# A fused DFT and two-layer MLP on one core: four float32 second stages for eight, two jobs moved to GpSimd, and the second transform one step sooner

## The chip, the core and the metric

The kernel runs on one core of a Trainium2 chip. The metric is the device time of one execution in microseconds (us). Before the change it is 877.92 us, the median of three runs between 877.84 and 877.99.

TensorE (PE in the profile; its weight loads are PEld) multiplies, VectorE (DVE) and ScalarE (ACT) do the elementwise work, GpSimd (POOL) does some more of it and issues a few DMAs, and SyncE (SP) issues the other DMAs. Each engine works through its own instructions in the order in which the program issued them; semaphores tie them together.

## The reference

```python
x: (4, 3008, 256) float32;  w_in: (256, 2048);  w_out: (2048, 256)
X = np.fft.fft(x, axis=1); X = np.fft.fft(X, axis=2)
t = X.real.reshape(12032, 256)
h = t @ w_in
g = h * (1.0 / (1.0 + np.exp(-h)))
return g @ w_out
```

## The kernel before, in words

The transform along the 256 features is folded into w_in at the start (lines 517 to 547), so that x has only to be transformed along the sequence. Symmetries of the real transform reduce that to `operand` (lines 251 to 326), which adds and subtracts folded rows of x, and `transform` (lines 328 to 358), one set of matrix products with cosine and sine tables (tiles te, to, t2). There are 16 such transforms, four for each of the four batches. `spread` (lines 368 to 388) takes the result of one out of PSUM into the tiles uvh and uvl, and copies one row of it over all 128 partitions with a DMA into the tile ub.

The MLP then runs over 13 chunks of columns: four of 376 or 378 columns and nine of 502. A chunk has 16 groups f of 128 hidden features. The main loop (lines 732 to 778) has one step n for each chunk and group; chunk 0 is steps 0 to 15, chunk 1 begins at step 16. A step issues, in this order:

- `first` (lines 404 to 412): six products into a PSUM tile pq, of which there are two;
- `second` of the group three steps back (LAG is 3): into four PSUM tiles acc;
- in some steps a transform (a "turn"), which takes a pq tile of its own;
- `act` (lines 417 to 436): three VectorE instructions (L421, L422, L423) from pq to the tile h, then the step's list `fills`, then Silu and a copy to gh on ScalarE;
- the step's list `after`, `rest` of the group before (L447 on VectorE, gl = h - gh), `spread` after a turn, the step's `plan`, and pieces of two work queues: `queue` (operands and `split_wo`) and `pool_queue` (`fold_sums`, `fold_diffs`, and the low part xl of an operand, L323).

The float32 numbers are multiplied as a high and a low part: three products for one (gh by woh, gh by wol, gl by woh; L464, L465, L471). In the first FULL = 8 groups of chunk 0 the second stage is made in plain float32 instead, as one product that the hardware runs in two passes (L462), without gh, gl and L447. The weights w_out for it are the four tiles `wo_f32`, which `split_wo` splits into high and low parts later (L123 on ScalarE, L125 on VectorE).

w_out comes as eight blocks q of 16-bit halves. `load_wo` fetches a block, `upper_wo` (ScalarE, L78) and `lower_wo` (VectorE, L82) put the halves together, and for the blocks that aren't needed in float32 `high_wo` (ScalarE, L115) and `low_wo` (VectorE, L118) split them. Block q is needed by the second stages of groups 2q and 2q+1. The lists `after` and `fills` (lines 722 to 730) say in which step each of these is issued.

The rows of x of the first batch are kept raw until `first_x1` (lines 195 to 211) adds their mirrored rows, the tiles minus; its last three additions (L210) run on VectorE in steps 2 and 3. `fold_diffs` (lines 213 to 247, GpSimd and ScalarE) uses the sums.

The order of work is written out by hand: `begins` gives the step in which the work on an operand begins, `turns` the step of its transform.

Of the kernel before, what the change touches and what calls it, by code (L numbers as in the profile page):

```python
# [24 lines left out]
F32 = mybir.dt.float32  # L25
# [7 lines left out]
ALU = mybir.AluOpType  # L33
PSUM = bass.MemoryType.PSUM

B, S, D, DFF = 4, 3008, 256, 2048
# [6 lines left out]
STARTS = [sum(CHUNKS[:j]) for j in range(len(CHUNKS))]  # L43
LAST = len(CHUNKS) - 1
LAG = 3
FULL = 8
NF = DFF // 128


# [1 line left out]
def fft_mlp(ctx, tc, x1, x2, x2_first, w_in, w_out, te, to, t2, t2f, rot1, rot2, dft, out):  # L51
    nc = tc.nc
    ctx.enter_context(tc.manual_schedule())
    tt = nc.vector.tensor_tensor
# [3 lines left out]
    fold_p = ctx.enter_context(tc.tile_pool(name="fold", bufs=1))  # L58
# [14 lines left out]
    def load_raw(t, block):  # L73
        nc.sync.dma_start(out=t[:, 1:1 + 8 * D].rearrange("p (c n) -> p c n", c=2), in_=block)

    def upper(dst, raw):
        flat = dst.rearrange("p c n -> p (c n)")
        nc.scalar.activation(flat.bitcast(F16)[:, 1::2], raw.bitcast(BF16)[:, 4:4 + 8 * D:4], AF.Copy)  # L78

    def lower(dst, raw):  # L80
        t = dst.rearrange("p c n -> p (c n)").bitcast(U32)
        stt(t, raw.bitcast(U32)[:, 1:1 + 4 * D:2], 13, t, op0=ALU.logical_shift_right, op1=ALU.bitwise_or)  # L82

    wo = [[wts.tile([128, 2, D], F32R, name=f"woh{f}") for f in range(NF // 2)], {}]
    wo_f32 = [wts.tile([128, 2, D], F32, tag="wof", name="wof", bufs=FULL // 2 + 1) for _ in range(FULL // 2)]
    for q in range(FULL // 2, NF // 2):
        wo[1][q] = wts.tile([128, 2, D], F32R, name=f"wol{q}")
# [4 lines left out]
    wo_raw, wo_wide = {}, {}  # L92

    def load_wo(q):
        if 3 <= q < 7:
            t = wr.tile([128, RAW], U16, tag="win", name="wo", bufs=4)
        else:
            tag = ("ri0", "xh", "xl")[q] if q < 3 else "ri1"
            t = (xs if tag[0] == "x" else fold_p).tile([128, RAW], U16, tag=tag, name="wo")
        wo_raw[q] = t  # L100
        load_raw(t, w_out[q * 256:(q + 1) * 256, :].bitcast(U16).rearrange("(f p) d -> p f d", p=128))

    def upper_wo(q):
        if q < FULL // 2:
            wo_wide[q] = wo_f32[q]
        else:
            wo_wide[q] = fold_p.tile([128, 2, D], F32, tag="half", name="wf", bufs=3)
            nc.gpsimd.memset(wo_wide[q], 0.0)
        upper(wo_wide[q], wo_raw[q])

    def lower_wo(q):
# [3 lines left out]
        nc.scalar.activation(wo[0][q], wo_wide[q], AF.Copy)  # L115

    def low_wo(q):
        tt(wo[1][q], wo_wide.pop(q), wo[0][q].bitcast(F32), op=ALU.subtract)  # L118

    def split_wo(q):  # L120
        wf, wh = wo_f32[q], wo[0][q]
        wl = wo[1][q] = wts.tile([128, 2, D], F32R, tag="wof", name="wol", bufs=FULL // 2 + 1)
        nc.scalar.activation(wh, wf, AF.Copy)  # L123
# [21 lines left out]
    def fold_tile(name, k, i):  # L145
        if (name, k, i) not in folded:
            folded[name, k, i] = fold_p.tile([128, 2, 2, D], F32, tag=f"{name}{k}", name=name)
        return folded[name, k, i]
# [22 lines left out]
    minus = {}  # L171
# [23 lines left out]
    def first_x1(h, x3, dd):  # L195
        g, sm = raw_x[0, 0, h], fold_tile("sm", 0, 0)[:, h]
        if h == 0:
            tt(g[:, 0:2], g[:, 0:2], minus[h, 0], op=ALU.add)
        tt(sm, g[:, 0:2], g[:, 2:4], op=ALU.add)
        if h:  # L200
            tt(sm, sm, minus[h, 0], op=ALU.add)
        yield
        tt(sm, sm, minus[h, 1], op=ALU.add)
        tt(dd, sm[:, 0], sm[:, 1], op=ALU.subtract)
        nc.scalar.activation(x3[:, h, ends], dd[:, ends], AF.Copy)
        tt(x3[:, h, 1:128], dd[:, 1:128], dd[:, 129:], op=ALU.add)
        tt(x3[:, 1 - h, 129:], dd[:, 1:128], dd[:, 129:], op=ALU.subtract)
        yield
        for j in range(1 - h, 2):
            tt(g[:, 2 * j:2 * j + 2], g[:, 2 * j:2 * j + 2], minus[h, j], op=ALU.add)  # L210
            yield

    def fold_diffs(k, i):
        tt = nc.gpsimd.tensor_tensor
        rot = rot_sb[k]
        gs = [raw_x.pop((k, i, h)) for h in range(2)]

        def differences(g):
            tt(g[:, 0:2], g[:, 0:2], g[:, 2:4], op=ALU.subtract)
            even, odd = g[:, 0:2, 1:128], g[:, 0:2, 129:]  # L220
            tt(g[:, 2:4, 1:128], even, odd, op=ALU.add)
            tt(g[:, 2, 129:], even[:, 1], odd[:, 1], op=ALU.subtract)
            tt(g[:, 3, 129:], odd[:, 0], even[:, 0], op=ALU.subtract)

        def turned(h, g):
            ri = fold_tile("ri", k, i)
            nc.scalar.activation(g[:, 2:4, ends], g[:, 0:2, ends], AF.Copy)
            for j in range(2):
                nc.scalar.activation(g[:, j], g[:, 3], AF.Copy, scale=rot[:, h, 1 - j:2 - j])
                nc.scalar.activation(ri[:, h, j], g[:, 2], AF.Copy, scale=rot[:, h, j:j + 1])  # L230

        def sums(h, g):
            ri = fold_tile("ri", k, i)
            for j, op in ((0, ALU.subtract), (1, ALU.add)):
                tt(ri[:, h, j], ri[:, h, j], g[:, j], op=op)  # L235

        differences(gs[0])
        yield 9
        differences(gs[1])
        yield 9  # L240
        turned(0, gs[0])
        yield 9
        sums(0, gs[0])
        turned(1, gs[1])
        yield 9
        sums(1, gs[1])
        ready.add(("ri", k, i, 128))
# [169 lines left out]
    def act(c, f, fill=()):  # L417
# [6 lines left out]
        for fn, q in fill:  # L424
            fn(q)
        if c == 0 and f < FULL:
            g = gp.tile([128, 2, CH], F32, tag=("gh", "gl")[f % 2], name="g")
# [12 lines left out]
    def rest(c, f):  # L440
        if c == 0 and f < FULL or (c, f) in rested:
            return
        rested.add((c, f))
        gh, gl, g = gs[c, f]
        n = chunks[c][3]
        for sg in signs(c, f):
            tt(gl[:, sg, :n], g[:, sg, :n], gh[:, sg, :n].bitcast(F32), op=ALU.subtract)  # L447
# [41 lines left out]
    queue, pool_queue = [], []  # L489
# [103 lines left out]
    x3 = xf[:, :768].rearrange("p (a d) -> p a d", a=3)  # L593
    x2_work = first_x2(x3)
    x1_work = [first_x1(h, x3, xf[:, 768 + 256 * h:1024 + 256 * h]) for h in range(2)]

    def product(a, i):
# [19 lines left out]
    for q in range(3):  # L617
        load_wo(q)
# [16 lines left out]
    product(0, 0)  # L635
    lower(wf32[4], win.pop(4))
    load_wo(3)
    project(4)
    next(x1_work[1])
# [7 lines left out]
    small(1)  # L647
    lower(wf32[5], win.pop(5))
    load_wo(4)
    project(5)  # L650
    first_spread = spread_first(po)
# [11 lines left out]
    upper(wf32[7], win[7])  # L663
    small(4)
    lower(wf32[7], win.pop(7))
    load_wo(6)


    def first_row():
# [8 lines left out]
    def at(j, f, fn, *a):  # L678
        j, f = j + f // NF, f % NF
        plan.setdefault((j, f), []).append((fn, a))  # L680
# [1 line left out]
    def add(q, name, work):  # L682
        q.append((name, work))

    turns, begins = {}, {1: (0, 4), 2: (1, 7), 3: (2, 0), 4: (2, 14), 5: (3, 3), 6: (3, 15)}
    for c in range(1, 4):
        turns[c - 1, 12] = c
    for b in range(1, B):
        j, c = 3 * b + 1, 4 * b
        for k, when in enumerate(((j - 1, 0 if b > 1 else 3), (j - 1, 12 if b > 1 else 11), (j, 8), (j + 1, 4))):  # L690
# [11 lines left out]
        at(j, f + 5 - (j < 3), add_x, k, i, *ps)  # L702
        at(j, f + 8 - (j < 3), add, pool_queue, (name, k, i), {"sm": fold_sums, "ri": fold_diffs}[name](k, i, *ps))

    at(0, 8, add, pool_queue, ("ri", 0, 0), fold_diffs(0, 0))
    for h in range(2):
        at(0, 11 + 2 * h, load_x, 1, 0, every, (h,))
        at(0, 15 + 2 * h, add_x, 1, 0, every, (h,))
# [4 lines left out]
    for b in range(1, B - 1):  # L713
        j = 3 * b + 1
# [5 lines left out]


    after, fills = {}, {}
    for q, n in enumerate((0, 1, 2, 3, 4, 5, 5, 7)):
        after.setdefault(n, []).append((upper_wo, q))
        fills.setdefault(n + 1, []).append((lower_wo, q))
        if q == 6:
            fills[n + 1].append((load_tables, q))
        if q >= FULL // 2:
            after.setdefault(n + 1, []).append((high_wo, q))
            fills.setdefault(n + 2, []).append((low_wo, q))  # L730

    for n in range(len(steps) + LAG):
        c, f = steps[min(n, len(steps) - 1)]
# [151 lines left out]
```

## Time and profile before

| | |
|---|---|
| median of three runs | 877.92 us |
| the profiled execution | 878.42 us |
| its span, first to last instruction | 876.7 us |
| mean granted TensorE clock | 1.000 of full speed |
| PE busy | 867.5 us (99%) |
| VectorE busy | 708.1 us (81%) |
| ScalarE busy | 507.0 us (58%) |
| GpSimd busy | 188.5 us (21%) |
| chain that ended last, by engine | PE 88%, DMA 4%, DVE 4%, ACT 2%, POOL 1% |

The shares are means over the whole span. Starts of matmuls are measured and their ends are modelled, so steps of TensorE are best read from start to start. A chain's share tells which engine each moment waited for; a wait that the profile shows in brackets behind an instruction is the idle time of its engine just before it, and who ended it.

### The profile page before, as it was taken

Reading aid. Unit: us, or ns where it says so; the run is one execution under the profiler, and the core shown is the slowest. Engines: PE = TensorE matmul, PEld = TensorE weight load, DVE = VectorE, ACT = ScalarE, POOL = GpSimd, SP = SyncE. Lnnn points to the kernel's source line nnn. Section 1 sums busy time; section 2 is a strip of 40 time slices with the busy share of each in tenths; the row PEclk is TensorE's granted clock in tenths of the full one; section 3 lists DMA queues with packets and bytes.
Section 4 is the critical chain, followed back from the end, with each engine's and each line's share of the span. In section 5 each row is a group of like instructions: output and inputs, shape, how many; then the busy total and the mean of one; then the engine's idle time right before and its main releaser. Section 6 shows DMA issues by size and latency. Waiting matters only on the chain.

```text
span 876.7 us, 11030 instructions
## 1 busy us (share of the span) xinstructions
PE 867.5 (99%) x4130; PEld 749.6 (86%) x4130; DVE 708.1 (81%) x1000; ACT 507.0 (58%) x644; POOL 188.5 (21%) x236
## 2 busy tenths in 40 slices
PE   8999999999999999999999999999999999999998
PEld 6779999999998888888888888888888888888886
DVE  5998988888897887889778777888877887777774
ACT  4676757555765565557566555557546556455544
POOL 3335531303522120243312310050200110000000
PEclk9999999999999999999999999999999999999999
DMA  9644343236131433224225201323011021200101
GB/s 337 229 160 73 97 71 54 37 58 93 8 97 37 68 85 58 37 17 106 41 19 135 9 1 49 56 48 57 1 7 50 0 10 48 10 0 4 44 1 47
DMA packets 22838, 51.71 MB, mean 59 GB/s; under 512 B 3585, under 2 KB 12161, under 8 KB 22401
## 3 DMA queue, kind: packets, MB, share of 16 engines
q1 hardware_dynamic: 19344, 37.58, 19.9%
q0 software_dynamic: 3440, 13.44, 7.7%
q8 instruction: 32, 0.52, 0.2%
q14 instruction: 22, 0.17, 0.1%
HBM read 35.77 MB, written 12.34 MB: 55 GB/s over the span
## 4 chain that ended last, share of the span: by engine, by line
PE 88%; DMA 4%; DVE 4%; ACT 2%; POOL 1%; issue 1%; SPq 0%; ACTq 0%; DVEq 0%
PE acc L471 19%; PE acc L465 19%; PE acc L464 19%; PE pq L410 9%; PE pq L412 9%; PE pq L411 9%; PE pq L341 5%; DMA ub<-row 1%; DMA x_t<-in_x_first_dram 1%; DMA win<-in_w_in_dram 1%; DMA wo<-in_w_out_dram 1%; POOL xl L323 1%; DVE h L421 1%; DVE h L422 1%; DVE wf L82 0%
## 5 line engine op out<-in xcount | busy, mean ns | idle before, releaser
L434 ACT ACTIVATE h<-h 128x1004 f32<-128x1004 f32 (+3 forms) x202 | 197.6, 978 | 304.3 <-DVE h L423 301.2
L464 PE MATMUL acc<-gh,woh 128*128 128x502 f32 (+2 forms) x800 | 299.4, 374 | 0.6 <-ACT o L479 0.6
L465 PE MATMUL acc<-gh,wol 128*128 128x502 f32 (+2 forms) x800 | 299.5, 374 | 0.0
L447 DVE TENSOR_TENSOR gl<-h,gh 128x1004 fp32r<-128x1004 f32 (+3 forms) x202 | 236.2, 1170 | 16.0 <-ACT gh L435 15.9
L421 DVE SCALAR_TENSOR_TENSOR h<-ub,a,pq 128x502 f32<-128x502 f32 (+2 forms) x208 | 144.8, 696 | 95.9 <-PE pq L412 89.4
L471 PE MATMUL acc<-gl,woh 128*128 128x502 f32 (+2 forms) x800 | 208.8, 375 | 0.0
L435 ACT ACTIVATE gh<-h 128x1004 fp32r<-128x1004 f32 (+3 forms) x202 | 197.6, 978 | 6.4
L465 PEld LDWEIGHTS acc<-gh,wol 128*128 128x128 f32 x800 | 151.1, 189 | 22.6
L464 PEld LDWEIGHTS acc<-gh,woh 128*128 128x128 f32 x800 | 150.4, 188 | 23.3 <-ACT o L479 0.9
L471 PEld LDWEIGHTS acc<-gl,woh 128*128 128x128 f32 x800 | 148.2, 188 | 22.9
L410 PE MATMUL pq<-uv,abh 128*128 128x502 f32 (+2 forms) x416 | 158.1, 380 | 0.1
L411 PE MATMUL pq<-uv,abh 128*128 128x502 f32 (+2 forms) x416 | 154.8, 372 | 0.0
L412 PE MATMUL pq<-uv,abl 128*128 128x502 f32 (+2 forms) x416 | 154.7, 372 | 0.0
L422 DVE TENSOR_TENSOR h<-h,pq 128x502 f32<-128x502 f32 (+2 forms) x208 | 132.7, 638 | 7.2
L423 DVE TENSOR_TENSOR h<-h,pq 128x502 f32<-128x502 f32 (+2 forms) x208 | 132.6, 637 | 7.2
L323 POOL TENSOR_TENSOR xl<-xf,xh 128x256 fp32r<-128x256 f32 x53 | 53.5, 1039 | 370.9 <-ACT xh L316 327.4
L410 PEld LDWEIGHTS pq<-uv,abh 128*128 128x128 f32 x416 | 78.2, 188 | 12.6 <-DVE h L423 0.7
L411 PEld LDWEIGHTS pq<-uv,abh 128*128 128x128 f32 x416 | 78.3, 188 | 11.9
L412 PEld LDWEIGHTS pq<-uv,abl 128*128 128x128 f32 x416 | 78.2, 188 | 11.2
L235 POOL TENSOR_TENSOR ri<-ri,raw 128x256 f32<-128x256 f32 x24 | 22.9, 971 | 55.3 <-ACT ri L230 55.1
L479 ACT ACTIVATE o<-acc 128x502 f32<-128x502 f32 (+2 forms) x52 | 27.6, 558 | 9.7 <-PE acc L471 7.6
L388 DVE TENSOR_TENSOR uv<-pq,uv 128x752 fp32r<-128x752 f32 (+4 forms) x21 | 14.5, 716 | 20.5 <-ACT row L384 20.4
(114 smaller groups left out, 476.7 us busy)
## 6 DMA issues: line engine op xcount, KB each, us to landing
raw<-in_x_dram SPq DMA_DIRECT2D x20, 512.0 KB, 5.5
raw<-in_x_dram POOLq DMA_DIRECT2D x18, 512.0 KB, 7.3
out_dram<-o SPq DMA_DIRECT2D x36, 251.0 KB, 2.1
win<-in_w_in_dram SPq DMA_DIRECT2D x8, 512.0 KB, 7.9
wo<-in_w_out_dram SPq DMA_DIRECT2D x8, 512.0 KB, 8.0
out_dram<-o SPq DMA_DIRECT2D x12, 188.0 KB, 2.4
ub<-row SPq DMA_DIRECT2D x8, 188.0 KB, 8.6
te<-in_te_dram POOLq DMA_DIRECT2D x1, 1128.0 KB, 5.9
```

Source lines behind the costliest of these rows:

```text
L410: nc.tensor.matmul(po, abh[:, i, fs], uvh[:, i, :n], start=True, stop=False)
L411: nc.tensor.matmul(po, abh[:, i, fs], uvl[:, i, :n], start=False, stop=False)
L412: nc.tensor.matmul(po, abl[:, i, fs], uvh[:, i, :n], start=False, stop=True)
L421: stt(p[:, :n], ub[:, :n], a128[f // 2][:, f % 2:f % 2 + 1], pq[:, 0, :n], op0=ALU.mult, op1=ALU.add)
L422: tt(h[:, 0, :n], p[:, :n], pq[:, 1, :n], op=ALU.add)
L423: tt(h[:, 1, :n], p[:, :n], pq[:, 1, :n], op=ALU.subtract)
L434: nc.scalar.activation(h[:, sg, :n], h[:, sg, :n], AF.Silu)
L435: nc.scalar.activation(gh[:, sg, :n], h[:, sg, :n], AF.Copy)
L447: tt(gl[:, sg, :n], g[:, sg, :n], gh[:, sg, :n].bitcast(F32), op=ALU.subtract)
L464: nc.tensor.matmul(po, wo[0][f // 2][:, f % 2, es], gh[:, sg, :n], start=f == 0, stop=False)
L465: nc.tensor.matmul(po, wo[1][f // 2][:, f % 2, es], gh[:, sg, :n], start=False, stop=False)
L471: nc.tensor.matmul(accs[c][i][:, :n], wo[0][f // 2][:, f % 2, es], gl[:, sg, :n], start=False, stop=f == NF - 1)
```

## The change

- FULL is 4: the second stages of groups 4 to 7 of chunk 0 are made of three products, with gh, gl and L447. Two blocks of w_out are kept in float32 and split later in place of four; six are split at once in place of four.
- `low_wo` (the subtraction L118) and the last three additions of `first_x1` (L210) run on GpSimd in place of VectorE. The clearing of the tiles for w_out's blocks, on GpSimd before and after, gets a place of its own, one step ahead of `upper_wo`.
- The blocks 6 and 7 of w_out are put together at steps 7 and 9 and the steps after them (before: 5 and 7). Block 6 is loaded in step 1, into another buffer, and no longer in the prologue.
- The work on operand 1 begins in step 2 (before: 4), and its transform is issued in step 11 (before: 12). The first `fold_diffs` is queued in step 9 (before: 8).

```diff
-FULL = 8
+FULL = 4
 def load_wo(q):
-    if 3 <= q < 7:
+    if 3 <= q < 6:
         t = wr.tile([128, RAW], U16, tag="win", name="wo", bufs=4)
     else:
-        tag = ("ri0", "xh", "xl")[q] if q < 3 else "ri1"
+        tag = {0: "ri0", 1: "xh", 2: "xl", 6: "ri0", 7: "ri1"}[q]
...
+def clear_wo(q):
+    wo_wide[q] = fold_p.tile([128, 2, D], F32, tag="half", name="wf", bufs=3)
+    nc.gpsimd.memset(wo_wide[q], 0.0)
+
 def upper_wo(q):
     if q < FULL // 2:
         wo_wide[q] = wo_f32[q]
-    else:
-        wo_wide[q] = fold_p.tile([128, 2, D], F32, tag="half", name="wf", bufs=3)
-        nc.gpsimd.memset(wo_wide[q], 0.0)
     upper(wo_wide[q], wo_raw[q])
...
 def low_wo(q):
-    tt(wo[1][q], wo_wide.pop(q), wo[0][q].bitcast(F32), op=ALU.subtract)
+    nc.gpsimd.tensor_tensor(wo[1][q], wo_wide.pop(q), wo[0][q].bitcast(F32), op=ALU.subtract)
...
     for j in range(1 - h, 2):
-        tt(g[:, 2 * j:2 * j + 2], g[:, 2 * j:2 * j + 2], minus[h, j], op=ALU.add)
+        p = g[:, 2 * j:2 * j + 2]
+        nc.gpsimd.tensor_tensor(p, p, minus[h, j], op=ALU.add)
         yield
...
     lower(wf32[7], win.pop(7))
-    load_wo(6)
...
-turns, begins = {}, {1: (0, 4), 2: (1, 7), ...}
+turns, begins = {}, {1: (0, 2), 2: (1, 7), ...}
 for c in range(1, 4):
-    turns[c - 1, 12] = c
+    turns[c - 1, 12 if c > 1 else 11] = c
...
-at(0, 8, add, pool_queue, ("ri", 0, 0), fold_diffs(0, 0))
+at(0, 9, add, pool_queue, ("ri", 0, 0), fold_diffs(0, 0))
...
-for q, n in enumerate((0, 1, 2, 3, 4, 5, 5, 7)):
+for q, n in enumerate((0, 1, 2, 3, 4, 5, 7, 9)):
     after.setdefault(n, []).append((upper_wo, q))
     fills.setdefault(n + 1, []).append((lower_wo, q))
-    if q == 6:
+    if q == 0:
+        fills[n + 1].append((load_wo, 6))
+    if q == 5:
         fills[n + 1].append((load_tables, q))
     if q >= FULL // 2:
+        fills.setdefault(n - 1, []).append((clear_wo, q))
         after.setdefault(n + 1, []).append((high_wo, q))
         fills.setdefault(n + 2, []).append((low_wo, q))
```

## Rows read from the trace of the kernel before

**Rows 1.** Stretches: us; busy PE, PEld, DVE, ACT, POOL; clock; DMA share, GB/s.
```profile
40.00:60.00 20.00, 20.00 (x80) 14.18 (x79) 19.51 (x43) 12.13 (x20) 3.01 (x7) 1.00 0.33 123
...
400.00:600.00 200.00, 200.00 (x910) 167.82 (x909) 160.09 (x207) 115.97 (x139) 48.23 (x52) 1.00 0.25 46
```
**Rows 2.** Timeline, weight loads that open steps: start us, duration us, instruction.
```profile
45.06 0.19 PEld L410 LDWEIGHTS pq<-uv,abh 128*128 128x128 f32 x1
...
48.60 0.19 PEld L410 LDWEIGHTS pq<-uv,abh 128*128 128x128 f32 x1
...
62.80 0.19 PEld L410 LDWEIGHTS pq<-uv,abh 128*128 128x128 f32 x1
...
66.04 0.19 PEld L410 LDWEIGHTS pq<-uv,abh 128*128 128x128 f32 x1
...
69.15 0.58 PEld L341 LDWEIGHTS pq<-te,xh 128*128 128x128 f32 x4
...
72.55 0.19 PEld L410 LDWEIGHTS pq<-uv,abh 128*128 128x128 f32 x1
```
**Rows 3.** Timeline of VectorE, steps 2 to 11.
```profile
37.16 0.68 DVE L82 SCALAR_TENSOR_TENSOR wof<-wo,wof 128x512 uint32<-128x512 uint32 x1
...
37.76 1.29 DVE L210 TENSOR_TENSOR raw<-raw,minus 128x512 f32<-128x512 f32 x2
...
41.85 0.61 DVE L421 SCALAR_TENSOR_TENSOR h<-ub,a,pq 128x376 f32<-128x376 f32 x1
...
43.54 0.70 DVE L82 SCALAR_TENSOR_TENSOR wof<-wo,wof 128x512 uint32<-128x512 uint32 x1
...
44.14 0.70 DVE L275 TENSOR_TENSOR sm<-sm 128x512 f32<-128x512 f32 x1
...
61.38 0.94 DVE L447 TENSOR_TENSOR gl<-h,gh 128x752 fp32r<-128x752 f32 x1
...
66.17 0.59 DVE L421 SCALAR_TENSOR_TENSOR h<-ub,a,pq 128x376 f32<-128x376 f32 x1
```
**Rows 4.** Timeline around the row's DMA and the start of chunk 1.
```profile
75.99 0.34 SPq L138 DMA_DIRECT2D raw<-in_x_dram  x1
...
76.42 0.55 SPq L385 DMA_DIRECT2D ub<-row  x1
...
86.13 0.61 DVE L421 SCALAR_TENSOR_TENSOR h<-ub,a,pq 128x378 f32<-128x378 f32 x1 [2.10 <-DMA ub<-row]
...
93.21 0.44 PE L464 MATMUL acc<-gh,woh 128*128 128x378 f32 x1 [0.59 <-ACT o L479]
```
**Rows 5.** Timeline of VectorE and GpSimd, three places where both work.
```profile
65.02 1.22 DVE L125 TENSOR_TENSOR wol<-wof,woh 128x512 fp32r<-128x512 f32 x1
...
70.31 1.28 POOL L219 TENSOR_TENSOR raw<-raw 128x512 f32<-128x512 f32 x1
...
70.68 1.71 DVE L447 TENSOR_TENSOR gl<-h,gh 128x752 fp32r<-128x752 f32 x1
...
71.67 1.31 POOL L221 TENSOR_TENSOR raw<-raw 128x254 f32<-128x254 f32 x1
...
206.01 1.29 POOL L219 TENSOR_TENSOR raw<-raw 128x512 f32<-128x512 f32 x1 [5.32 <-DMA raw<-in_x_dram]
207.38 1.06 POOL L221 TENSOR_TENSOR raw<-raw 128x254 f32<-128x254 f32 x1
...
206.66 1.19 DVE L275 TENSOR_TENSOR sm<-sm 128x512 f32<-128x512 f32 x1
207.87 1.13 DVE L278 TENSOR_TENSOR sm<-sm 64x512 f32<-64x512 f32 x1
```
**Rows 6.** Timeline of GpSimd: the clearing of w_out's tiles, and xl.
```profile
36.14 1.45 POOL L108 MEMSET wf<- 128x512 f32 x3
...
61.52 5.32 POOL L323 TENSOR_TENSOR xl<-xf,xh 128x256 fp32r<-128x256 f32 x5 [6.10 <-ACT xh L316]
```
**Rows 7.** DMA issues up to 130 us: count, KB, us from issue to landing.
```profile
to<-in_to_dram POOLq DMA_DIRECT2D x1, 1128.0 KB, 9.2
```

More of the change, by code (lines that the diff above doesn't have):

```diff
@@ L683, in add @@
         q.append((name, work))
-    turns, begins = {}, {1: (0, 4), 2: (1, 7), 3: (2, 0), 4: (2, 14), 5: (3, 3), 6: (3, 15)}
+    turns, begins = {}, {1: (0, 2), 2: (1, 7), 3: (2, 0), 4: (2, 14), 5: (3, 3), 6: (3, 15)}
     for c in range(1, 4):
-        turns[c - 1, 12] = c
+        turns[c - 1, 12 if c > 1 else 11] = c
     for b in range(1, B):
```

## The prediction, as put on record before the change was run

> **What bounds the kernel now.** I read the page first, then the stretches, then the timeline of the start. In the middle of the run TensorE is busy without a gap, 200.00 of 200 us [rows 1], so what the first 100 us gain or lose moves the end one for one. The change touches only steps 1 to 13. There two engines are full at once: TensorE 20.00 of 20 us, VectorE 19.51 [rows 1]. So the question is which of them sets the pace afterwards.
>
> TensorE from start to start [rows 2]: a step with a float32 second stage takes 48.60 - 45.06 = 3.54 us; the first step of three products 66.04 - 62.80 = 3.24; the next 69.15 - 66.04 = 3.11; a transform 72.55 - 69.15 = 3.40. These float32 steps follow each other without a stall.
>
> VectorE is late all the while but not too late. There are two pq tiles, so `first` of step n+2 needs the three VectorE instructions of `act`(n), the trio, to be done. The trio of step 4 begins at 41.85 and L82 follows at 43.54: a trio is 1.69 us. From the end of trio 2 (37.16) to the start of trio 11 (66.17) VectorE has 29.0 us [rows 3], and its work fills them: eight trios 13.5; seven L82 at 0.6 (37.16 to 37.76) 4.2; three L210 1.8; operand 1 3.9 (an L275 of 0.70, the rest smaller); four L118 at 0.6 2.4; two L447 at 0.94 and one L125 together some 3.1 [rows 3, 5].
>
> **The change part by part.**
>
> *Float32 stages.* Steps 7 to 10 go from float32 to three products. Step 7 now holds the switch (3.54 to 3.24), steps 8 to 10 take 3.11, and step 11 no longer holds the switch: 0.30 + 3 x 0.43 + 0.13 = **1.7 us less** on TensorE, if nothing holds it up [rows 2].
>
> *The row's DMA.* At the start of chunk 1 VectorE waits 2.10 us for ub, because SP issued the row's DMA at 76.42, behind a load of x that had waited for GpSimd until 75.99 [rows 4]. That delay travels through ScalarE to the copies of acc, and TensorE stands still for 0.59 us at 93.21 [rows 4]. With the transform in step 11, `spread` is issued before that step's load of x, and the row goes out a step earlier, ahead of it. The wait of 2.10 is less than a step of 3.11, so it goes: **0.6 us less**. If SP held the row up after all, this would be 0.
>
> *VectorE's work.* Out: three L210 (1.8), four L118 (2.4), and the wait inside the one L125 (0.5). In: four L447 (rest of groups 4 to 7) at 0.94, 3.7. Operand 1 only moves two steps up inside the stretch, and of the splits L125 one stays in it. So 29.0 - 4.7 + 3.7 = 28.0, and trio 11 would begin at 65.2, end at 66.9. TensorE, running free, wants `first` of step 12 at 72.55 - 3.11 - 1.7 = 67.7. VectorE's margin is then only 0.8 us.
>
> *The two engines in each other's way.* This is the unknown that decides. The rows show it exactly: L447 at 70.68 takes 1.71 us in place of 0.94; GpSimd's L219 had begun at 70.31 and ended at 71.59, and 0.80 later L447 is done. Then GpSimd's L221 waits in its turn for L447 [rows 5]. When both have instructions queued they alternate: L219 from 206.01, then L275 (1.19 in place of 0.70), then L221, then L278 (1.13) [rows 3, 5]. The trios, which read PSUM, keep their length beside GpSimd. So each GpSimd instruction that reads two tiles can hold up one VectorE instruction that reads two, by up to its own length: 1.29 us for 512 columns, as L219 at 206.01 [rows 5].
>
> The change puts eight such instructions of 512 columns into the stretch (three additions, `low_wo` of blocks 2 to 6), brings the five L323 forward into it (5.32 us together, [rows 6]), and the first L219 and its followers come into it as well: some 17 us of GpSimd work in 28 us.
>
> Upper price, by a walk through the queues in order of issue. GpSimd is free for the additions at about 36.9: in the old order its clears begin at 36.14 [rows 6] and one now stands ahead of the additions. So L82 of step 2, due at 37.16, waits 1.0; L275 behind it waits for the second addition, 1.1. L82 of step 5 meets `low_wo`(3), 0.6. L447 of group 6 meets L323, 0.5; L82 of step 8 meets `low_wo`(5), 0.8; the L447s of groups 7 and 8 meet an L323 and `low_wo`(6), 0.5 each; the instructions of step 10 meet the first `fold_diffs`, 0.6. With 0.4 for L82 of step 5 waiting for ScalarE, which now has to copy gh as well, the sum is **6.0 us**. Lower price: before, over the L323s and the first `fold_diffs` (9.5 us of GpSimd work by undisturbed lengths), VectorE lost 0.54 in L125 and 0.77 in L447 [rows 5], 14%; 14% of 17 us is **2.4 us**. I take the middle, 4.2, because in this stretch VectorE has twice as many two-tile instructions beside its trios as in that of the low price, but the walk lets every meeting fall badly.
>
> *At nothing.* The loads of the tables wait for L82 of block 5 as before, now one L82 earlier; the last of the two that the transform reads lands 9.2 us after its issue [rows 7], near 62 to 64 us, and the transform comes at 64.3 at the soonest: if the cover goes, it is a few tenths. Block 6 of w_out loads in step 1 and is used in step 8. ScalarE has 12.13 of 20 us busy [rows 1]; four copies to gh and two more early splits fit, save for the 0.4 above. GpSimd's new place for L108 lies in its idle time. `load_x` stays behind GpSimd's `fold_diffs`, with many steps before operand 2.
>
> *The sum.* Trio 11 begins at 65.2 + 4.2 = 69.4 and ends, with its semaphore, at 71.2. TensorE had the same point (13 steps less one, transform done) at 72.55 - 3.11 = 69.44: 1.7 us late; the 1.7 us gained on TensorE are inside that, eaten by the wait. `first` of step 13 needs the pq tile of the transform, which `spread` frees only after ScalarE has finished two groups: 0 to 0.6, I take 0.3. Less 0.6 for the row: 1.7 + 0.3 - 0.6 = +1.4. On the profiled execution, span 876.7 and 878.42 in all, that makes 878.1 and 879.8; the median lies 0.5 below that execution, so **879.3 us**. With the lower price it is -0.4, 877.5; with the upper +3.5, 881.4.
>
> [...] The rows above show two-tile VectorE instructions and GpSimd's held up by each other. [...]
>
> **The rivals.**
>
> *Every meeting falls badly* (the lock at its full price): 6.0 us, so +3.5 and 881.4 us; if the last piece of operand 1 in step 2 also waits for the third addition, 1.1 more, 882.5. For it: both of VectorE's queued pairs in the trace alternate with GpSimd. Against: many L323 and L219 met only trios, at no cost.
>
> *Faster: the meetings fall under the trios.* VectorE's margin of 0.8 us decides: if the lock costs less than that, TensorE runs free through steps 7 to 15 and both gains stay, -1.7 - 0.6 = -2.3, 875.6 us. For it: a trio of 1.69 covers a whole GpSimd instruction of 1.29, and `low_wo` is released by ScalarE, often just when VectorE begins a trio. Against: the three additions wait for nothing and stand right before L82 and L275.
>
> *A light price*, 0.8 to 3 us: from -2.3 to +0.2, not to be told from no change for most of it.
>
> *The change doesn't do what it says* at the row: 0.6 us more in any of these; it changes none of their signs.
>
> **How the numbers follow.** About 0.2% (1.76 us) is what a measurement here can tell from no change. My forecast, a price of 3 to 5.2 us (+0.2 to +2.4), has a chance of 0.41: 0.28 of it within 0.2%, 0.13 slower. The full price, +2.4 to +4.6, has 0.25, all slower. The light price has 0.15, nearly all within. The trios cover it: 0.19, nearly all faster. So faster 0.18, same 0.44, slower 0.38. The range goes from the free run, 875.5, to a full price somewhat over the walk, 882.0; the forecast's own is 878.1 to 880.3.
>
> **What would show it.** In the timeline after: steps of TensorE of 3.24 and 3.11 from step 7 on with no stall would show the free run; stalls before L410 of steps 5, 8, 9, 11 and 12, each ended by a trio, the forecast. L82 and L275 of step 2 at 1.2 to 1.8 us in place of 0.69 would show the lock; trio 11 beginning near 65 (free), 69.4 (forecast) or 71 (full price) tells the cases apart. The first L421 of chunk 1 without a wait for ub, and L464 of step 19 without one for acc, would show the row. [...]

## The result and the profile after

The changed kernel takes **883.27 us** (883.06 to 883.71), beside 877.95 (877.84 to 878.25) for the kernel before on the same chip: a ratio of 1.0061, with a 95% interval of 1.0043 to 1.0078. That is 5.3 us slower. The prediction was 879.3, and its range ended at 882.0. The profiled execution took 883.41 us, with a span of 881.6 in place of 876.7. In the text below, lines of `first` and of the trio move by two (L410 is L412, L421 to L423 are L423 to L425), L447 is L449, L210 is L212, L118 is L119, L125 is L126, L323 is L325 and L388 is L390; L82 stays. In the changed kernels with the additions back on VectorE, and in the kernel before with the additions on GpSimd, they mostly move by one.

The two stretches that [rows 1] showed, with the 20 us between them (us, then busy PE, PEld, DVE, ACT, POOL, granted clock, DMA share, GB/s); first those 20 us before, then all three after:

```profile
60.00:80.00 20.00, 20.00 (x122) 18.84 (x121) 17.94 (x27) 15.33 (x27) 16.14 (x17) 1.00 0.27 82
```

```profile
40.00:60.00 20.00, 17.59 (x74) 13.63 (x73) 19.30 (x37) 12.79 (x21) 9.58 (x14) 0.91 0.13 41
60.00:80.00 20.00, 16.95 (x106) 15.89 (x105) 18.70 (x24) 13.77 (x22) 18.37 (x18) 1.00 0.41 136
400.00:600.00 200.00, 200.00 (x907) 167.42 (x906) 162.01 (x212) 117.45 (x138) 47.40 (x51) 1.00 0.27 51
```

TensorE, which had been busy for 20.00 of 20 us in both, is now busy for 17.59 and then 16.95. VectorE is about as full as before. GpSimd has gone from 3.01 to 9.58 us in the first. In the middle of the run TensorE is still without a gap, so the loss stands in the first 90 us. The weight loads of TensorE that open a step, and the idle time before them, as in [rows 2]; first that of step 16 before, then those after, from step 5 to step 16:

```profile
81.90 0.19 PEld L410 LDWEIGHTS pq<-uv,abh 128*128 128x128 f32 x1
```

```profile
44.27 0.19 PEld L412 LDWEIGHTS pq<-uv,abh 128*128 128x128 f32 x1 [3.01 <-DVE h L425]
...
49.31 0.19 PEld L412 LDWEIGHTS pq<-uv,abh 128*128 128x128 f32 x1
...
52.86 0.19 PEld L412 LDWEIGHTS pq<-uv,abh 128*128 128x128 f32 x1
...
56.10 0.19 PEld L412 LDWEIGHTS pq<-uv,abh 128*128 128x128 f32 x1
...
59.18 0.19 PEld L412 LDWEIGHTS pq<-uv,abh 128*128 128x128 f32 x1
...
66.83 0.19 PEld L412 LDWEIGHTS pq<-uv,abh 128*128 128x128 f32 x1 [1.23 <-DVE h L425]
...
74.24 0.19 PEld L412 LDWEIGHTS pq<-uv,abh 128*128 128x128 f32 x1 [0.90 <-DVE h L425]
...
78.95 0.19 PEld L412 LDWEIGHTS pq<-uv,abh 128*128 128x128 f32 x1 [1.69 <-DVE uv L390]
...
88.19 0.19 PEld L412 LDWEIGHTS pq<-uv,abh 128*128 128x128 f32 x1
```

The step lengths are the ones forecast: the step with the switch takes 56.10 - 52.86 = 3.24 us, the next 59.18 - 56.10 = 3.08. But the steps begin late: TensorE waits for a trio at 44.27, 66.83 and 74.24, and for `spread` (L390) at 78.95. The step of 44.27 also takes 5.04 us in place of 3.54. Step 16 begins at 88.19; before, it began at 81.90. That is 6.3 us late. At step 20 it is 5.3 (100.61 in place of 95.31), because TensorE's wait for acc in chunk 1 [rows 4] has gone, and at the end of this execution 4.9 (881.6 - 876.7). VectorE's timeline says why, as [rows 3] did before:

```profile
37.03 4.57 DVE L82 SCALAR_TENSOR_TENSOR wof<-wo,wof 128x512 uint32<-128x512 uint32 x1
41.52 0.68 DVE L277 TENSOR_TENSOR sm<-sm 128x512 f32<-128x512 f32 x1
...
42.46 0.59 DVE L423 SCALAR_TENSOR_TENSOR h<-ub,a,pq 128x376 f32<-128x376 f32 x1
...
50.53 1.27 DVE L82 SCALAR_TENSOR_TENSOR wf<-wo,wf 128x512 uint32<-128x512 uint32 x1 [0.28 <-ACT wf L78]
...
72.43 0.59 DVE L423 SCALAR_TENSOR_TENSOR h<-ub,a,pq 128x376 f32<-128x376 f32 x1
...
75.96 2.09 DVE L449 TENSOR_TENSOR gl<-h,gh 128x752 fp32r<-128x752 f32 x1 [0.70 <-ACT gh L437]
```

The row at 37.03 is L82 of step 2: 4.57 us for an instruction that took 0.68. It is shown as busy, not as idle: the wait is inside the instruction. Trio 3 begins at 42.46 (before: 38.97), and trio 11 at 72.43 (before: 66.17). GpSimd at the same time:

```profile
36.84 2.52 POOL L212 TENSOR_TENSOR raw<-raw,minus 128x512 f32<-128x512 f32 x2
39.31 0.52 POOL L105 MEMSET wf<- 128x512 f32 x1
39.79 1.25 POOL L212 TENSOR_TENSOR raw<-raw,minus 128x512 f32<-128x512 f32 x1
...
49.95 1.29 POOL L119 TENSOR_TENSOR wol<-wf,woh 128x512 fp32r<-128x512 f32 x1 [1.48 <-ACT woh L116]
```

The last of the three additions ends at 41.04, and L82, which stood ready from 37.03, is over at 41.60, 0.56 later: it waited through all three and through the clearing between them. The meeting at 49.95 is of the small kind: the L82 that begins at 50.53 ends 0.56 after that subtraction. "The lock" in the prediction and "the port" in the expectations are its author's names for this waiting of VectorE and GpSimd on each other: the traces show the waiting (here 4.57 us for an L82 of 0.68), not its cause.

At the start of chunk 1 the row's DMA and the first trio, as in [rows 4]:

```profile
77.00 0.55 SPq L387 DMA_DIRECT2D ub<-row  x1
```

```profile
89.60 0.61 DVE L423 SCALAR_TENSOR_TENSOR h<-ub,a,pq 128x378 f32<-128x378 f32 x1
```

No load of x stands ahead of the row any more, the wait of 2.10 us for ub has gone, and so has TensorE's for acc.

### The profile page after: what moved, and what is told of

It reads as the page before. It is cut to its first block, busy times and chain, and to the rows that moved or that the text cites. A ratio compares the mean times of both kernels' runs of the same rounds, so it can differ in the third digit from the quotient of the medians.

```text
span 881.6 us, 11078 instructions
## 1 busy us (share of the span) xinstructions
PE 868.0 (98%) x4146; PEld 752.5 (85%) x4146; DVE 711.6 (81%) x995; ACT 510.5 (58%) x648; POOL 202.5 (23%) x245
## 4 chain that ended last, share of the span: by engine, by line
PE 89%; DVE 2%; issue 1%; ACT 0%; DVEq 0%
PE acc L473 19%; PE acc L467 19%; PE acc L466 19%; PE pq L412 9%; PE pq L413 9%; PE pq L414 9%; PE pq L343 5%; DVE h L423 0%; DVE h L424 0%; DVE h L425 0%; DVE gl L449 0%; DVE sm L280 0%; DVE uv L390 0%; DVE sm L277 0%; ACT h L436 0%
## 5 line engine op out<-in xcount | busy, mean ns | idle before, releaser
L436 ACT ACTIVATE h<-h 128x1004 f32<-128x1004 f32 (+3 forms) x206 | 200.9, 975 | 306.5 <-DVE h L425 303.2
L467 PE MATMUL acc<-gh,wol 128*128 128x502 f32 (+2 forms) x816 | 304.7, 373 | 0.0
L466 PE MATMUL acc<-gh,woh 128*128 128x502 f32 (+2 forms) x816 | 304.5, 373 | 0.0
L449 DVE TENSOR_TENSOR gl<-h,gh 128x1004 fp32r<-128x1004 f32 (+3 forms) x206 | 240.9, 1170 | 15.1 <-ACT gh L437 15.1
L423 DVE SCALAR_TENSOR_TENSOR h<-ub,a,pq 128x502 f32<-128x502 f32 (+2 forms) x208 | 144.7, 696 | 97.6 <-PE pq L414 93.2
L473 PE MATMUL acc<-gl,woh 128*128 128x502 f32 (+2 forms) x816 | 212.1, 374 | 0.0
L437 ACT ACTIVATE gh<-h 128x1004 fp32r<-128x1004 f32 (+3 forms) x206 | 200.9, 975 | 6.5
L467 PEld LDWEIGHTS acc<-gh,wol 128*128 128x128 f32 x816 | 153.9, 189 | 22.6
L466 PEld LDWEIGHTS acc<-gh,woh 128*128 128x128 f32 x816 | 153.4, 188 | 22.2
L473 PEld LDWEIGHTS acc<-gl,woh 128*128 128x128 f32 x816 | 151.0, 188 | 23.2 <-DVE gl L449 0.2
L412 PE MATMUL pq<-uv,abh 128*128 128x502 f32 (+2 forms) x416 | 157.2, 378 | 5.5 <-DVE h L425 4.1
L425 DVE TENSOR_TENSOR h<-h,pq 128x502 f32<-128x502 f32 (+2 forms) x208 | 132.6, 638 | 7.2
L325 POOL TENSOR_TENSOR xl<-xf,xh 128x256 fp32r<-128x256 f32 x53 | 53.6, 1040 | 363.2 <-ACT xh L318 303.9
L412 PEld LDWEIGHTS pq<-uv,abh 128*128 128x128 f32 x416 | 78.1, 188 | 18.4 <-DVE h L425 5.7
L390 DVE TENSOR_TENSOR uv<-pq,uv 128x752 fp32r<-128x752 f32 (+4 forms) x21 | 14.5, 715 | 21.0 <-ACT row L386 21.0
```

The lines of the kernel that those rows point to most:

```text
L412: nc.tensor.matmul(po, abh[:, i, fs], uvh[:, i, :n], start=True, stop=False)
L423: stt(p[:, :n], ub[:, :n], a128[f // 2][:, f % 2:f % 2 + 1], pq[:, 0, :n], op0=ALU.mult, op1=ALU.add)
L425: tt(h[:, 1, :n], p[:, :n], pq[:, 1, :n], op=ALU.subtract)
L436: nc.scalar.activation(h[:, sg, :n], h[:, sg, :n], AF.Silu)
L437: nc.scalar.activation(gh[:, sg, :n], h[:, sg, :n], AF.Copy)
L466: nc.tensor.matmul(po, wo[0][f // 2][:, f % 2, es], gh[:, sg, :n], start=f == 0, stop=False)
```

## The experiments

The experiments ran on several chips; beside them the kernel before took 878.14 to 878.17 us, and 877.95 beside the changed kernel, so a difference of 0.2 us between two runs says nothing.

**Two theories.** Theory 1: VectorE sets the pace over the whole stretch; the three additions hold it up, and trio 11 and L390 are where TensorE is bound in the end. What TensorE loses in between (the stall at 44.27, the slow step behind it) would be absorbed by the later waits. Theory 2, its rival: the loss is the single stall at 44.27, 2.4 us between two products (3.01 between two weight loads), and the 1.5 us of the slow step; without the additions on GpSimd nearly all would come back.

**The additions back on VectorE, in the changed kernel.**

```diff
-            p = g[:, 2 * j:2 * j + 2]
-            nc.gpsimd.tensor_tensor(p, p, minus[h, j], op=ALU.add)
+            tt(g[:, 2 * j:2 * j + 2], g[:, 2 * j:2 * j + 2], minus[h, j], op=ALU.add)
```

> The changed kernel with the three additions of raw rows back on VectorE; all else as changed. Theory 1 (VectorE's chain from step 2 to the transform sets the end; the stall of TensorE at step 5 and the clock drop behind it are absorbed): VectorE gets back the 4.0 us that L82 stood still and pays 1.8 us for three additions, so trio 11 begins 2.0 us sooner (70.4 in place of 72.4) and the time is about 881.3 us. Theory 2 (the stall of 2.9 us at step 5 and the 1.5 us of slow clock are lost for good): both vanish, about 878.9 us. Either way L82 of step 2 is back at 0.69 us.

Measured: 881.96 us (881.63 to 882.18), ratio 1.0043 (1.0028 to 1.0058). The stall at step 5 has shrunk to 0.33 us and the slow step has gone, but trio 11 is still late:

```profile
36.88 0.68 DVE L82 SCALAR_TENSOR_TENSOR wof<-wo,wof 128x512 uint32<-128x512 uint32 x1
...
71.22 0.60 DVE L422 SCALAR_TENSOR_TENSOR h<-ub,a,pq 128x376 f32<-128x376 f32 x1
```

Trio 11 moves from 72.43 to 71.22, and the time by 1.3 us. That is near the 881.3 of theory 1; the 878.9 of theory 2 is 3 us away. In place of the one long stall there are several of 0.3 to 1.8 us. Beside the rest of the change, moving the additions made the kernel slower by 1.3 us.

**The subtractions of `low_wo` back on VectorE, in the changed kernel.**

```diff
-        nc.gpsimd.tensor_tensor(wo[1][q], wo_wide.pop(q), wo[0][q].bitcast(F32), op=ALU.subtract)
+        tt(wo[1][q], wo_wide.pop(q), wo[0][q].bitcast(F32), op=ALU.subtract)
```

> The changed kernel with w_out's six subtractions back on VectorE; all else as changed. Theory 1: VectorE pays five more instructions of 0.6 us before trio 11 (3.0) and is rid of about 1.6 us of meetings with them, so 1.4 us later: about 884.7 us. Theory 2: the same stall at step 5, no change: 883.3. Rival (these subtractions on GpSimd are what costs): faster than the changed kernel by 1 us or more.

Measured: 885.72 us (885.24 to 886.33), ratio 1.0088 (1.0071 to 1.0105): 2.45 slower than the changed kernel, with trio 11 later by 2.8:

```profile
75.26 0.60 DVE L423 SCALAR_TENSOR_TENSOR h<-ub,a,pq 128x376 f32<-128x376 f32 x1
```

So this part of the change did help, beside the rest of it.

**The additions on GpSimd, in the kernel before.** The edit is the first diff turned round.

> The kernel before with the three additions alone on GpSimd. If GpSimd keeps the shared port through its queued additions, L82 of step 2 lasts 4.6 us again, TensorE stands still some 2 us at step 5, the clock falls, and the time is 880 to 881.5 us. If the 4.6 us had another cause in the changed kernel (operand 1 two steps sooner, the loads of w_out), L82 lasts 1.2 to 1.8 us and the time is 877.5 to 878.5.

Measured: 878.96 us (878.16 to 879.63) beside 878.15, ratio 1.0008 (0.9999 to 1.0018).

```profile
37.04 3.38 DVE L82 SCALAR_TENSOR_TENSOR wof<-wo,wof 128x512 uint32<-128x512 uint32 x1
```

```profile
36.12 3.74 POOL L211 TENSOR_TENSOR raw<-raw,minus 128x512 f32<-128x512 f32 x3
```

```profile
42.14 0.19 PEld L411 LDWEIGHTS pq<-uv,abh 128*128 128x128 f32 x1 [0.90 <-DVE h L424]
```

It is the same kind of wait: L82 is held through three additions, until 40.4 (3.38 us in place of 0.68). But VectorE no longer has the additions (1.8 us) to do itself, so its net loss is about 1 us, and before the transform TensorE stalls only once, by 0.90. The cost is 0.8, less than was expected, and its interval just reaches no change: here VectorE has margin to take the rest.

**The transform a step sooner, in the kernel before.**

```diff
-    turns, begins = {}, {1: (0, 4), ...
+    turns, begins = {}, {1: (0, 2), ...
-        turns[c - 1, 12] = c
+        turns[c - 1, 12 if c > 1 else 11] = c
-    at(0, 8, add, pool_queue, ("ri", 0, 0), fold_diffs(0, 0))
+    at(0, 9, add, pool_queue, ("ri", 0, 0), fold_diffs(0, 0))
```

> The kernel before with the second transform and its operand alone moved up (transform in step 11, operand from step 2, first differences queued in step 9). The wait for ub at chunk 1 (2.1 us on VectorE, 0.6 to 0.9 on TensorE) goes: 877.1 us if VectorE can take the operand in steps 2 and 3 without making TensorE wait; if it cannot, trio 3 and 4 come 1 to 2 us later and eat it: 878.

Measured: 879.60 us (879.16 to 880.59), ratio 1.0016 (1.0007 to 1.0026). A miss: the waits for ub and for acc have gone, yet it is 1.45 slower. (The profiled execution is the slowest of ten; 0.9 us of it lie ahead of step 2.) The operand's work in steps 2 to 4 makes trios late (stalls of 0.35 and 0.73), and xl now meets the subtractions:

```profile
56.46 3.60 DVE L118 TENSOR_TENSOR wol<-wf,woh 128x512 fp32r<-128x512 f32 x2
```

```profile
56.22 2.14 POOL L323 TENSOR_TENSOR xl<-xf,xh 128x256 fp32r<-128x256 f32 x3
```

```profile
61.80 0.19 PEld L410 LDWEIGHTS pq<-uv,abh 128*128 128x128 f32 x1 [1.38 <-DVE h L423]
```

Two L118, 1.28 us together when nothing holds them, take 3.60; the trio behind them is late, and TensorE stalls by 1.38 for it.

**The row alone.** In the kernel before, the two loads of x for transform (1, 0) are issued one step later and in neighbouring steps, so that the first stands behind the row's DMA.

```diff
-        at(0, 11 + 2 * h, load_x, 1, 0, every, (h,))
+        at(0, 12 + h, load_x, 1, 0, every, (h,))
```

> The kernel before with one load of x (the first of the second half's rows) issued in step 12 in place of 11, behind the row's DMA on SP. The row goes out when ScalarE has it, 1.6 us sooner; VectorE's wait for ub at chunk 1 falls from 2.1 to about 0.5 us and TensorE's wait for acc goes. If that wait is worth what the prediction said, 0.6 to 0.9 us less than before: about 877.3. If it is hidden elsewhere or the later load costs as much, no change.

Measured: **877.33 us** (876.52 to 877.91) beside 878.17, ratio 0.9990 (0.9982 to 0.9999).

```profile
74.62 0.55 SPq L385 DMA_DIRECT2D ub<-row  x1
75.86 3.90 SPq L138 DMA_DIRECT2D raw<-in_x_dram  x2
```

```profile
84.00 0.61 DVE L421 SCALAR_TENSOR_TENSOR h<-ub,a,pq 128x378 f32<-128x378 f32 x1
```

The row goes out at 74.62, ahead of the loads, the wait of 2.10 at chunk 1 has gone, and no step of TensorE behind it waits. This one line is worth 0.8 us (0.1 to 1.6 by the interval), and it is faster than both kernels, if by little.

**The clock.** In the changed kernel TensorE is kept busy through the stall of step 5 by ten more products, into columns of acc that nobody reads.

```diff
+        if n == 5:
+            for _ in range(10):
+                nc.tensor.matmul(accs[0][0][:, 376:512], wo_f32[0][:, 0, :128], wo_f32[0][:, 0, :136], start=False, stop=False)
```

> The changed kernel with ten small float32 products between the stages of steps 4 and 5, into columns of the acc banks that nothing reads, so that TensorE is busy while it waits for trio 3. Theory 1 (VectorE's chain sets the end): the granted clock stays at its upper level in steps 5 and 6, the step from 44.27 takes 3.5 us in place of 5.04, and the time doesn't move: 883 us, within 0.5. Theory 2 (the slow clock is lost for good): 1.5 us less, 881.8.

Measured: 883.24 us (882.91 to 883.80), ratio 1.0059 (1.0043 to 1.0074). The stretches (columns as above), first of the changed kernel, then with the filling:

```profile
42.00:44.00 2.00, 0.00 (x0) 0.00 (x0) 1.93 (x5) 0.00 (x0) 0.00 (x0) 1.00 0.00 0
44.00:46.00 2.00, 1.73 (x7) 1.45 (x8) 2.00 (x7) 1.67 (x3) 0.24 (x1) 0.86 0.00 0
46.00:48.00 2.00, 2.00 (x5) 1.13 (x4) 1.93 (x4) 0.91 (x4) 1.94 (x4) 0.50 0.00 0
48.00:50.00 2.00, 2.00 (x8) 1.31 (x7) 1.93 (x6) 1.97 (x4) 0.47 (x3) 0.79 0.01 4
```

```profile
46.00:48.00 2.00, 2.00 (x9) 1.37 (x8) 1.93 (x6) 0.92 (x4) 1.89 (x5) 1.00 0.00 0
```

```profile
43.91 0.19 PEld L412 LDWEIGHTS pq<-uv,abh 128*128 128x128 f32 x1 [0.29 <-DVE h L425]
...
47.26 0.19 PEld L412 LDWEIGHTS pq<-uv,abh 128*128 128x128 f32 x1
...
55.02 0.19 PEld L412 LDWEIGHTS pq<-uv,abh 128*128 128x128 f32 x1 [0.95 <-DVE h L425]
```

The granted clock stays at 1.00, the step takes 3.35 in place of 5.04, and the time is unchanged: TensorE arrives sooner at step 8 and waits there for VectorE (0.95 at 55.02, where there was no stall). The slow step is absorbed, and theory 2 is out.

That the filling is what kept the clock up is not shown. In the run with the subtractions back on VectorE, TensorE did nothing from 42 to 44 us either, without any filling, and its granted clock stayed at 1.00 (columns as above):

```profile
42.00:44.00 2.00, 0.00 (x0) 0.00 (x0) 1.93 (x5) 0.00 (x0) 0.00 (x0) 1.00 0.00 0
...
46.00:48.00 2.00, 2.00 (x8) 1.15 (x7) 1.93 (x4) 0.91 (x4) 0.00 (x0) 1.00 0.00 0
```

Its step 5 took 3.34 us (44.33 to 47.67). In the variant with a tiny addition (below) the gap was about the same (2.3 us between two products, 2.4 in the changed kernel), step 5 took 3.35 us, and TensorE waited for 1.01 at step 8: the slow step is absorbed there too. Each of these is the profile of one execution.

**FULL = 4 alone, in the kernel before.**

```diff
-FULL = 8
+FULL = 4
```

> The kernel before with FULL = 4 alone: four second stages of chunk 0 in three products in place of float32, nothing moved to GpSimd, the transform where it was. Theory 1 (VectorE sets the pace as soon as it gets more to do): four L447 (0.94 each and 0.09 of waiting for h) and two L118 (0.6) more before trio 11, so it begins 5 us later, at 71, and TensorE waits for it before the transform: 881.5 to 882. Theory 3 (TensorE's own work counts): 1.7 us less than before, 876.4.

Measured: 882.96 us (882.54 to 883.87), ratio 1.0057 (1.0040 to 1.0074): nearly the whole loss, with nothing moved to GpSimd.

```profile
50.24 0.60 DVE L421 SCALAR_TENSOR_TENSOR h<-ub,a,pq 128x376 f32<-128x376 f32 x1
...
54.98 0.60 DVE L421 SCALAR_TENSOR_TENSOR h<-ub,a,pq 128x376 f32<-128x376 f32 x1
...
72.04 0.59 DVE L421 SCALAR_TENSOR_TENSOR h<-ub,a,pq 128x376 f32<-128x376 f32 x1
```

```profile
61.52 0.19 PEld L410 LDWEIGHTS pq<-uv,abh 128*128 128x128 f32 x1 [1.68 <-DVE h L423]
```

```profile
40.00:60.00 20.00, 18.73 (x88) 14.99 (x86) 19.70 (x40) 14.36 (x23) 4.05 (x9) 1.00 0.24 85
```

VectorE is busy for 19.70 of 20 us, and from 50.24 to 54.98 its own work in a step is 4.74 us: a trio, L118, two L82, an L447 and two pieces of the operand. TensorE's step of three products is 3.24 at most, so it waits. Trio 11 is nearly as late (72.04) as in the changed kernel.

**The subtractions on GpSimd, in the kernel before.** The edit is the second diff turned round.

> The kernel before with w_out's four subtractions alone on GpSimd. VectorE is rid of 2.4 us and pays for some meetings, and it had a margin of 1.4 to 2 us there that TensorE doesn't feel: no change by theory 1, 877.8 to 878.6. If each meeting with the port is paid by TensorE, 1 to 2 us more.

Measured: 879.28 us (878.63 to 879.89) beside 878.14, ratio 1.0013 (1.0004 to 1.0022). No change was expected; it is 1.1 slower. One of the moved subtractions stands between the L323, and where L125 had taken 1.22 [rows 5] it now takes 1.78; the next L447 takes 1.75 in place of 1.06. That L447 makes the next trio late by 0.7 (it begins 3.51 us behind the one before it, in place of 2.82), and with it `spread`, for which TensorE now waits:

```profile
76.17 0.19 PEld L410 LDWEIGHTS pq<-uv,abh 128*128 128x128 f32 x1 [1.03 <-DVE uv L388]
```

**Both jobs back on VectorE, in the changed kernel** (the first two diffs together).

> The changed kernel with both the three additions and w_out's six subtractions back on VectorE: what is left is FULL = 4 and the earlier transform. By theory 1 and the two runs that undid one each (881.96 and 885.72 against 883.27), the two effects add: about 884.4 us. If GpSimd's work is what the change costs, near 880.

Measured: 883.21 us (882.88 to 883.30), ratio 1.0057 (1.0042 to 1.0072), where 884.4 was expected; trio 11 begins at 73.21. With this the change can be read as a ladder: 878.15 before; 882.96 with FULL = 4; 883.21 with the sooner transform and the small moves (blocks 6 and 7 later, the clearing's place) as well; 881.96 with the subtractions on GpSimd; 883.27 with the additions there too. The two moves to GpSimd together bring nothing. They also depend on each other: with the additions moved first, the steps are 883.21, 885.72 and 883.27.

**How many GpSimd instructions VectorE waits for.** Three variants of the changed kernel, one execution each. First, each addition cut into two of 256 columns:

```diff
-            p = g[:, 2 * j:2 * j + 2]
-            nc.gpsimd.tensor_tensor(p, p, minus[h, j], op=ALU.add)
+            for p, m in zip((g[:, 2 * j], g[:, 2 * j + 1]), (minus[h, j][:, 0], minus[h, j][:, 1])):
+                nc.gpsimd.tensor_tensor(p, p, m, op=ALU.add)
```

> The changed kernel with each of the three additions on GpSimd as two of 256 columns. If GpSimd keeps the port only between long instructions of the same kind, L82 of step 2 gets its turn after the first short one and lasts about 1.3 us; then trio 3 begins about 40 to 41 and the time is about 881 us. If GpSimd passes the port to itself whatever the length, L82 lasts 4.6 us or somewhat more, and the time is 883 to 884.

Measured: 883.42 us.

```profile
37.56 1.08 DVE L82 SCALAR_TENSOR_TENSOR wof<-wo,wof 128x512 uint32<-128x512 uint32 x1
38.56 1.23 DVE L277 TENSOR_TENSOR sm<-sm 128x512 f32<-128x512 f32 x1
```

Now L82 gets its turn after one half: it takes 1.08 us. But the two instructions behind it are each held as well (L277 takes 1.23 in place of 0.68), trio 3 begins at 40.58 in place of 42.46, and the time is the same. In this execution step 2 began 0.5 us later (37.56 in place of 37.03) and step 16 0.3 sooner (87.89 in place of 88.19), so some 0.8 us were gained from step 2 on, where 2 were expected. The shorter instructions changed where VectorE waited, and later meetings took most of the gain (the L286 at 44.07 takes 1.36 us in place of 0.28).

Second, a tiny GpSimd addition in the prologue, in case the first arithmetic on that engine is special:

```diff
+    nc.gpsimd.tensor_tensor(once[0:1, 1800:1864], ones[:, :64], ones[:, 64:], op=ALU.add)
```

> The changed kernel with one tiny GpSimd addition (1 x 64) in the prologue, so that the three additions are no longer GpSimd's first arithmetic. If L82's 4.6 us come from something that GpSimd does at its first arithmetic, L82 lasts 1.2 to 1.8 us and the time is about 881; if not, nothing changes: 4.6 us and 883 us.

Measured: 884.57 us, with L82 of step 2 still at 4.49 us. That idea falls. Half of the 1.3 us to the changed kernel lies ahead of step 2 (L82 at 37.68 in place of 37.03); the other half comes behind step 16, and the trace of one execution shows no cause.

Third, the additions one in each of the steps 2, 3 and 4:

```diff
-        if n in (2, 3):
-            for work in x1_work:
-                next(work, None)
+        if n in (2, 3, 4):
+            next(x1_work[n > 2], None)
```

> The changed kernel with GpSimd's three additions one in each of steps 2, 3 and 4, not two in step 2 and one in step 3. Each then stands alone, so none of VectorE's instructions can wait for more than one: L82 of step 2 lasts 1.2 to 1.8 us in place of 4.57, and those of steps 3 and 4 up to 1.9. Theory 1: trio 3 begins 2.5 us sooner, some of it is paid back in steps 3 and 4, and the time is 881 to 882.5 us.

Measured: 882.78 us.

```profile
37.30 3.34 DVE L82 SCALAR_TENSOR_TENSOR wof<-wo,wof 128x512 uint32<-128x512 uint32 x1
```

```profile
37.11 1.27 POOL L212 TENSOR_TENSOR raw<-raw,minus 128x512 f32<-128x512 f32 x1
38.33 0.52 POOL L105 MEMSET wf<- 128x512 f32 x1
38.81 1.28 POOL L212 TENSOR_TENSOR raw<-raw,minus 128x512 f32<-128x512 f32 x1
```

A miss again: at most 1.8 us was expected for L82. GpSimd's second addition is free to run at once (it doesn't wait for its step), and L82 is held through the first, the clearing and the second.

## Why the prediction was wrong

**The sign and the path were right, the size was beyond even the full-price rival.** The forecast was a loss of 1.4 us by VectorE's waits for GpSimd, which make trio 11 late; the loss is 5.3, and such waits do make trio 11 late. But nearly the same loss comes without the moves to GpSimd (4.8 with FULL = 4 alone), as VectorE then does itself what it waits for here. The two rows named as the test, trio 11 and L82 of step 2, came out beyond the worst case: 72.43 where 71 was the full price, and 4.57 where 1.2 to 1.8 was written.

**Float32 stages: right in size, not cashed.** The steps are 3.24 and 3.08 where 3.24 and 3.11 were taken. (A float32 product stands in the trace as two L462: eight for the four products of a step, 2.24 us from 46.39 to 48.63 before.) The 1.7 us went into TensorE's waits, as the sum said they would.

**The row's DMA: right.** The wait for ub has gone, and with it the one for acc; the row alone gives 0.8 where 0.6 was taken. But the way there, moving the transform, costs more than that: 1.45 us slower in the kernel before. The prediction put the sooner operand at no cost, as it stays inside the stretch. What it missed is that the operand takes the margin of the single early steps, and that xl comes under the subtractions.

**The sum for the full price has a slip.** By the prediction's own terms a price of 6.0 is 1.8 above 4.2, so +3.2 and 881.1, where it has +3.5 and 881.4; the larger number would fit with the wait for uv at the top of its 0 to 0.6. The result is beyond both.

**VectorE's work: right.** From 37.03, the end of trio 2, the 28.0 us of the prediction lead to 65.0. The rest of the way to 72.43, **7.4 us**, is waiting.

**The two engines in each other's way: the step that failed.** 4.2 us was taken, with 2.4 and 6.0 as its bounds. Of the measured 7.4, L82 of step 2 alone is 3.9 (41.52 - 37.03, less 0.60), where the walk had 1.0, and 1.1 more for the L275 behind it. The walk let the engines alternate, as the queued pairs of [rows 5] did; nowhere in the trace of before is a VectorE instruction held for much over 1 us (the longest L447 takes 2.23, its median is 1.20). Here L82 was held through three additions and a clearing. Of the other 3.5, L82 of step 5 is 0.9 (0.3 of it for ScalarE); the rest is meetings of 0.1 to 0.7 at steps 7 to 10. For these the walk's single prices were about right: it had 3.9 for everything behind step 2, counting 0.4 for ScalarE. So the walk's list, not the middle between it and 14%, was the better estimate, and its one wrong entry was the first. The low bound came from L323s that mostly met trios.

The prediction took one GpSimd instruction as the most that one VectorE instruction can be held up by, with 1.29 us as its length. The waits of L82 end alike, 0.55 to 0.56 us after the last GpSimd instruction that it waited for; but that was the subtraction alone for the row at 50.53, and the second or third addition for the rows that took 4.57, 3.38 and 3.34. The trios did keep their length, as the prediction says: in the kernel before, beside the five L323 from 61.52 on and the L219 at 66.81, L421 took 0.59 to 0.61 us, L422 and L423 0.55 each.

**The wait for uv: mis-sized.** 0.3 was taken for the step after the transform, within 0 to 0.6; it is 1.6 (78.95 - 74.24 = 4.71 for a step of 3.11). L449 at 75.96, which takes 2.09 us in place of 0.94 beside a subtraction and was late by ScalarE before that, stands ahead of L390. Trio 11 at 72.43 is 3.0 us later than forecast, and with 1.3 here that makes 4.3; the row's gain, 0.8 in place of 0.6, takes 0.2 back. So the terms give 4.1 of the 4.0 between 879.3 and 883.27.

**What the prediction didn't see at all** is how the parts compare. FULL = 4 costs 4.8 us by itself, since VectorE gets four more L447 and two more L118 in a stretch where it was already full [rows 1]. The moves to GpSimd then take three additions and six subtractions off VectorE, 9 x 0.6 = 5.4 us, and the time stays: from the end of trio 2 to trio 11 it is 35.1 us with FULL = 4 alone (36.91 to 72.04) and 35.4 after (37.03 to 72.43). The time in which VectorE no longer computes, it now waits. The prediction had both numbers in one sum, and so a margin of 0.8 us that only an undisturbed VectorE has.

**Open.** Why VectorE waits through several GpSimd instructions in some places (additions of 512 columns, with a clearing between them, 4.57 us; the L323 at 56.22 in one experiment, 3.60 for two L118) and through one in others (halves of 256 columns, 1.08; L219 before L275 in [rows 5], 1.19) isn't settled. Halving the additions changed it; their being GpSimd's first arithmetic didn't matter. Length alone doesn't decide: L323s of 256 columns, as at 56.22, let an L118 through after one of them (1.11 us, at 65.13) in the run with FULL = 4 alone. No run separates the rest.

## What to carry to other kernels

Work taken off a full VectorE and given to GpSimd can come back as waiting: here 5.4 us of it came back as 5.7 (35.4 us to trio 11 in place of 35.1, with 5.4 less to do). What VectorE issues at that moment seems to decide, though no run isolates it: the additions, ready just as VectorE came to L82 and L277, cost 1.3 to 2.5 us with FULL = 4 (1.3 beside the moved subtractions, 2.5 without), while the subtractions, released one by one by ScalarE, gained 1.3 to 2.5; in the kernel before, where VectorE had some margin, four of these subtractions cost 1.1. Before a saving on one of two full engines, ask what it adds to the other (1.7 us off TensorE cost 4.8 us here), and where a DMA is late because of a neighbour in its queue, move the neighbour, not the whole chain of work ahead of it.

## What the runs showed of the hardware

- L82, a VectorE instruction that reads two tiles, neither of them in PSUM, waited through several GpSimd instructions: 3.9 us through three additions and a clearing, 2.7 through three additions, and 2.7 through two with a clearing between. In these traces it shows as a long busy instruction, not as idle time.
- After TensorE had done nothing from 42 to 44 us in the changed kernel, its granted clock was 0.86, 0.50 and 0.79 in the next three stretches of 2 us, and one step took 5.04 us in place of 3.54. After the same gap it stayed at 1.00 in the profiles of two variants, whose step took 3.34 and 3.35 us, and it stayed at 1.00 with the gap filled by more products. So a gap like this may or may not cost a slow step. The time was the same with and without it (883.24 and 883.27), since TensorE was not the bound there.
